# Moving the scaling and splitting of softplus results to a later place among the attention tiles

## The chip, the cores and the metric

The kernel runs on one core of a Trainium2 chip. The metric is the device time of one execution in microseconds (us). Engines are named as in the profile: PE (TensorE matmuls), PEld (TensorE weight loads), DVE (VectorE), ACT (ScalarE), POOL (GpSimd), SP (SyncE, which issues the DMAs). All of them run their own instructions in order and meet through semaphores.

## What is computed

Attention with a threshold, and behind it a feed-forward layer with softplus, all in float32 at the interface:

```
scores = scale * q @ k.T                      # 8 x 8 heads, 576 x 576, head size 64
thresh = max(scores, axis=-1) - tau
attn   = exp(where(scores >= thresh, scores, -1e9) - max)   # then divided by its row sum
x      = (attn @ v), heads side by side        # 4608 x 512
h = x @ w_in                                   # 4608 x 2048
g = max(h, 0) + log1p(exp(-abs(h)))            # softplus
out = g @ w_out                                # 4608 x 512
```

## The kernel before, in words

**Attention.** A unit is a pair of heads (32 units); a unit has 9 tiles of 128 query rows, so there are 288 tiles, counted here from 0 (tile 204 is the seventh of unit 22). A tile goes through: scores on PE (4 matmuls of 128x288 in float32, `scores`), the negated row maximum on DVE (`row_max`, tile `negm`), the exponentials on ACT with the threshold right behind them (`exps`, tiles `e_all` and `thr`), the mask on DVE (`mask`, written back to `e_all`, which also gives the row sums), and then the split of the weights into two float16 halves: the upper half on POOL (`weights_hi`) and the lower half on DVE (`weights_lo`), both in the tile that the profile calls `h`. These go through a DMA transpose (`weights_T`) and meet the values on PE (`values`, tile `pv`), whose result is copied by ACT and added by DVE into `xp`. There are two score banks (`SB = 2`): the scores of a tile can start only when the mask of the tile two before it has read its bank.

**Feed-forward.** The rows are taken in 10 chunks, eight of 512 rows and two of 256 (`chunks`; the last two form the tail, behind the attention). A chunk has 16 hidden blocks of 128 columns; `hidden` makes one by 12 matmuls from `xh`, `xl` and `w_i`. Two blocks at a time (a pair) go to `softplus` (line 737): ACT loads the softplus table, makes two softplus activations out of PSUM into `st`, and scales each in place by a power of two (`u.sg`). POOL then splits each `st` into `gh` and `gl` (`parts_of`, line 763, by `halves`, line 183): four POOL instructions a pair, called the parts here; the profile names their results `g`. `project` multiplies the parts by `w_o` into `o`, and DVE or ACT adds `o` into `acc`. A matmul chunk has 8 pairs; in the stretch where attention and feed-forward run together the first of a chunk's seven ordinary pairs stands alone, and the other six come in three twos, about 8.6 us apart within a two.

**The order.** Each tile writes its instructions by a string, `PAT = "RemhlTfpSxfvwp"`: row maximum (R, of the tile two ahead), exponentials (e, two ahead), mask (m, one ahead), upper half (h, one ahead), lower half (l, this tile), transposes (T), a share of the feed-forward matmuls (f), a point (p), scores (S, three ahead), extras of the unit (x: queries and keys of the next unit, values of the last), again f, v, w, and a second point (p). The first p is the middle of a tile. `defer(n, f)` puts a step at the n-th point from now; `now["p"]` counts points and is odd in a middle. From tile 36 on, ACT, DVE and POOL keep exactly the order in which the code writes their instructions (class `Queue`, whose calls are all recorded at line 160); PE and SP are ordered by the scheduler, by its own estimate of when an instruction can start.

A pair's `softplus` is written at the point after its last hidden matmul (`HD[0] = 1`), its scalings right with it, and its parts one point later (`HD[1] = 1`). While weights are still being prepared (`prep`), and for the last pair of a chunk (`u.n in waits`), the parts are put off further.

Of the kernel before, what the change touches and what calls it, by code (L numbers as in the profile page):

```python
# [54 lines left out]
HD = (1, 1)  # L55
# [11 lines left out]
def tile_kernel(ctx: ExitStack, tc: tile.TileContext, q, k, v, tau, w_in, w_out, out):  # L67
# [76 lines left out]
    now = {"p": 0, "tile": 0}  # L144
# [570 lines left out]
    def hidden(u, fc):  # L715

        g, f = divmod(fc, 4)
        need("i", g)
        h_scales(u, g)
        n = TC // u.T  # L720
        i = fc % n
        if i == 0:
            u.bank = ps_g.tile([P, TC], F32, tag="g", name=f"h_{u.n}_{fc}")
        bank = u.bank
        e = slice(f * P, (f + 1) * P)
        for cc in range(NCC):
            for m, (a, x) in enumerate(((0, u.h), (0, u.l), (1, u.h))):
                nc.tensor.matmul(bank[:, i * u.T:(i + 1) * u.T], wi[g, cc][:, a, e], x[cc], start=(cc == 0 and m == 0),  # L728
                                 stop=(cc == NCC - 1 and m == 2))
                if cc == NCC - 1 and m == 2 and i == n - 1:  # L730
                    u.full.append((fc + 1 - n, bank))
                    if len(u.full) == PAIR:
                        full, u.full = u.full, []
                        defer(HD[0], lambda: softplus(u, full))
                yield u.T / 512

    def softplus(u, full):


        ts, last_ = [], None  # L740
        with tc.high_priority(SPP):
            for fc, bank in reversed(full):
                t = fpool.tile([P, TC], F32, tag="st", bufs=NST, name=f"st_{u.n}_{fc}")
                i = act.activation(t, bank, AF.Softplus, scale=u.ch[:, fc // 4:fc // 4 + 1]).ins
                if last_ is not None:
                    tc.add_manual_dep(i, last_.name, mybir.DependencyInfo(
                        mybir.DependencyClass.NoSync, mybir.DependencyReason.DATA), reason="one table load")
                last_ = i
                ts.append((fc, t))
            for fc, t in reversed(ts):  # L750
                act.activation(t, t, AF.Copy, scale=u.sg[:, fc // 4:fc // 4 + 1])
        def parts():
            if u.n in waits:
                waits[u.n].append(parts)
                return
            for n, (fc, t) in enumerate(reversed(ts)):
                defer(n if prep else 0, lambda fc=fc, t=t: parts_of(u, fc, t))
        defer(HD[1], parts)

    waits = {}  # L760
    later_g = [0]

    def parts_of(u, fc, t):

        home, tags, bufs = (fpool, ("gh", "gl"), NG)
        if u.tail:
            spare = [("kT", "kT", 2), ("qT0", "qT1", 1), ("nat", "nat", 2), ("vt", "vt", 2)]
            i = later_g[0] % (NG + len(spare))
            later_g[0] += 1
            if i >= NG:  # L770
                *tags, bufs = spare[i - NG]
                home = apool
        gh, gl = [home.tile([P, TC], F16, tag=tags[i], bufs=bufs, name=f"g{i}_{u.n}_{fc}") for i in range(2)]
        halves(gh, gl, t)
        for i in range(TC // u.T):
            c = slice(i * u.T, (i + 1) * u.T)
            u.g[fc + i] = (gh[:, c], gl[:, c])
# [113 lines left out]
    def defer(n, f):  # L891
        if n == 0:
            f()
        else:
            later.append((now["p"] + n, f))
# [19 lines left out]
    for n, (main, b, from_) in enumerate(spans):  # L915
        u = Chunk()
# [16 lines left out]
    prep = []  # L933
    for kind, g in WL:
        for m in range(4):
            n = len(prep)
# [167 lines left out]
```

## Time and profile before

| what | value |
|---|---|
| median of 3 runs (lowest to highest) | 1295.86 us (1295.76 to 1297.07) |
| the profiled execution, its own time | 1297.34 us |
| its span from first to last instruction | 1295.6 us |
| busy: PE, DVE, ACT, POOL | 95%, 71%, 69%, 69% |
| mean granted TensorE clock | 0.996 |
| softplus pairs | 72 (144 activations) |

The span is 1.7 us shorter than the profiled execution's own time; the rest lies around the instructions. The median of the runs is 1.5 us below the profiled execution. In the rows of a timeline stand the start in us, the duration in us, the engine, line, operation, result and inputs, shapes and count, and in brackets the idle time before it with what ended it. In the rows of waits stand the waiting engine and tile, what it waited for, then us in total, times and the longest. In the tables of stretches stand the stretch, its length, and each engine's busy us.

### The profile page before, as it was taken

What the parts mean: (1) busy time and instruction counts of PE and PEld (TensorE: products, weight loads), DVE (VectorE), ACT (ScalarE), POOL (GpSimd) and SP (SyncE); (2) the same over time, 40 slices, a digit from 0 to 9 for tenths busy, and PEclk for the clock granted to TensorE, in tenths of its full rate; (3) what the DMA queues carried; (4) which work ended last, traced back from release to release, by engine and by line L of the source; (5) the groups of instructions that cost most, each with busy time, mean ns of one, the idle gap of its engine ahead of it and who ended that gap; (6) DMA issues with size and microseconds to landing.
All of it is one profiled execution on the core that took longest, in us unless ns stands there. A gap on an engine that the chain in (4) does not pass through costs nothing.

```text
span 1295.6 us, 21809 instructions
## 1 busy us (share of the span) xinstructions
PE 1230.8 (95%) x7173; PEld 745.1 (58%) x7173; DVE 925.7 (71%) x1735; ACT 900.2 (69%) x1723; POOL 893.1 (69%) x970
## 2 busy tenths in 40 slices
PE   5999988888999999999999999999999999999998
PEld 4655545455665565656565655666657755554455
DVE  5889878989777887878777977786677676640111
ACT  5877887877777777777777787768676767744321
POOL 2466788888876787778766886687667777564332
PEclk9999999999999999999999999999999999999999
DMA  4545357755876787768767776676557555420010
GB/s 130 160 143 148 111 129 169 177 116 125 185 144 146 137 178 154 154 139 175 145 146 145 165 153 147 144 149 155 130 122 165 124 123 108 100 65 17 1 41 17
DMA packets 368738, 167.92 MB, mean 130 GB/s; under 512 B 320208, under 2 KB 346224, under 8 KB 368624
## 3 DMA queue, kind: packets, MB, share of 16 engines
q1 hardware_dynamic: 368624, 166.52, 57.5%
q8 instruction: 57, 0.93, 0.3%
q14 instruction: 57, 0.47, 0.1%
HBM read 56.62 MB, written 10.63 MB: 52 GB/s over the span
## 4 chain that ended last, share of the span: by engine, by line
PE 35%; ACT 15%; POOL 10%; DVE 8%; issue 7%; DMA 5%; SPq 1%; POOLq 0%; DVEq 0%; ACTq 0%
PE o L792 14%; PE h L728 12%; PE s L493 5%; ACT st L160 5%; ACT L160 5%; POOL g L160 4%; PE pv L608 3%; DVE h L160 2%; ACT e_all L160 2%; POOL h L160 2%; DVE negm L160 2%; DVE e_all L160 2%; POOL xl L160 1%; DMA eT<-h 1%; DVE acc L160 1%
## 5 line engine op out<-in xcount | busy, mean ns | idle before, releaser
L792 PE MATMUL o<-w_o,g 128*128 128x512 f16 x1728 | 405.0, 380 | 2.1 <-DVE xp L160 1.2
L728 PE MATMUL h<-xh,w_i 128*128 128x512 f16 (+1 forms) x1280 | 361.3, 359 | 6.7 <-ACT sums_i L160 3.6
L160 POOL TENSOR_SCALAR h<-e_all 128x576 f16<-128x576 f32 x243 | 223.9, 924 | 112.3 <-DVE e_all L160 108.6
L160 ACT ACTIVATE e_all<-s,negm 128x576 f32<-128x576 f32 x288 | 213.6, 742 | 124.8 <-DVE negm L160 121.8
L160 DVE TENSOR_REDUCE negm<-s 128x1 f32<-128x576 f32 x288 | 215.2, 747 | 87.4 <-PE s L493 86.3
L160 DVE SCALAR_TENSOR_TENSOR e_all<-s,thr,e_all 128x576 f32<-128x576 f32 x288 | 232.8, 809 | 62.2 <-ACT thr L160 61.3
L728 PEld LDWEIGHTS <-w_i 128*128 128x128 f16 x1920 | 178.8, 98 | 170.2 <-issue 14.3
L792 PEld LDWEIGHTS <-g 128*128 128x128 f16 x1728 | 159.5, 98 | 174.1 <-issue 3.5
L160 DVE SCALAR_TENSOR_TENSOR h<-e_all,h 128x576 f16<-128x576 f32 x243 | 229.4, 944 | 26.5 <-POOL h L160 26.1
L728 PE MATMUL h<-xl,w_i 128*128 128x512 f16 (+1 forms) x640 | 230.3, 360 | 1.2 <-POOL xl L160 1.0
L160 POOL TENSOR_SCALAR g<-st 128x512 f16<-128x512 f32 x144 | 97.9, 680 | 165.8 <-ACT st L160 154.2
L160 POOL TENSOR_TENSOR g<-st,g 128x512 f16<-128x512 f32 x144 | 172.6, 1199 | 12.0
L493 PE MATMUL s<-kT,q 128*128 128x288 f32 x768 | 154.5, 329 | 16.5 <-DVE e_all L160 11.8
L160 DVE SCALAR_TENSOR_TENSOR acc<-o,c,acc 128x512 f32<-128x512 f32 x108 | 80.2, 742 | 124.6 <-PE o L792 124.2
L160 ACT ACT_TABLE_LOAD x119 | 152.7, 1283 | 2.1
L160 ACT ACTIVATE st<-h,c 128x512 f32<-128x512 f32 x144 | 91.1, 684 | 79.9 <-PE h L728 79.2
L493 PEld LDWEIGHTS s<-kT,q 128*128 128x128 f32 x768 | 116.4, 192 | 48.6 <-DVE e_all L160 31.5
L608 PE MATMUL pv<-eT,vt 128*128 128x288 f16 x972 | 139.9, 287 | 3.4 <-DVE xp L160 2.5
L493 PE MATMUL s<-kT,qT 128*128 128x288 f32 x512 | 106.8, 329 | 4.2 <-DVE e_all L160 3.8
L608 PEld LDWEIGHTS <-vt 128*128 128x128 f16 x972 | 88.7, 98 | 37.1 <-issue 5.0
L160 ACT COPY xp<-pv 64x288 f32<-64x288 f32 (+3 forms) x133 | 50.5, 383 | 78.8 <-PE pv L608 74.8
L160 ACT ACTIVATE st<-st,c 128x512 f32<-128x512 f32 x144 | 96.1, 714 | 2.3
(118 smaller groups left out, 1504.1 us busy)
## 6 DMA issues: line engine op xcount, KB each, us to landing
q<-q SPq DMA_DIRECT2D x62, 192.0 KB
kn<-in_k_dram SPq DMA_DIRECT2D x32, 256.0 KB
qn<-in_q_dram SPq DMA_DIRECT2D x32, 256.0 KB
vn<-in_v_dram SPq DMA_DIRECT2D x32, 256.0 KB
wc_i<-in_moe_w_in_dram SPq DMA_DIRECT2D x16, 512.0 KB
wc_o<-in_moe_w_out_dram SPq DMA_DIRECT2D x16, 512.0 KB
qT<-qT SPq DMA_DIRECT2D x62, 128.0 KB
out_dram<-acc SPq DMA_DIRECT2D x14, 512.0 KB
```

The costliest lines, as they stand in the source:

```text
L160: i = getattr(self.eng, name)(*args, **kwargs)
L493: nc.tensor.matmul(sp[:, hf, 0:HS], lhs, s.kT[j][:, hf * HS:(hf + 1) * HS], start=(m == 0), stop=(m == len(parts) - 1))
L608: nc.tensor.matmul(o[:, 0:HS], s.vt[:, a, :], s.eT[j][:, b, x0:x0 + HS], start=(n == 0), stop=(n == 2 * NC))
L728: nc.tensor.matmul(bank[:, i * u.T:(i + 1) * u.T], wi[g, cc][:, a, e], x[cc], start=(cc == 0 and m == 0), stop=(cc == NCC - 1 and m == 2))
L792: nc.tensor.matmul(o, u.g[fc][m // 2][:, sl], wo[fc][:, m % 2, :], start=(n == 0), stop=(n == 3 * QF - 1))
```

## The change

For a pair outside the tail, after the preparation of weights, and not among those that are put off, the scalings are no longer written with the softplus activations. They and the parts are both put at the next middle of a tile: one point on when the softplus was written at the end of a tile, two when it was written in a middle. A function `scaled` now holds the scalings.

```diff
                 last_ = i
                 ts.append((fc, t))
+
+        def scaled():
             for fc, t in reversed(ts):
                 act.activation(t, t, AF.Copy, scale=u.sg[:, fc // 4:fc // 4 + 1])
+
         def parts():
             if u.n in waits:
                 waits[u.n].append(parts)
                 return
             for n, (fc, t) in enumerate(reversed(ts)):
                 defer(n if prep else 0, lambda fc=fc, t=t: parts_of(u, fc, t))
-        defer(HD[1], parts)
+        if prep or u.tail or u.n in waits:
+            scaled()
+            defer(HD[1], parts)
+            return
+
+        n = 1 + now["p"] % 2
+        defer(n, scaled)
+        defer(n, parts)
```

In the built program 48 of the 72 pairs are moved. The instructions and their number are the same on ACT, POOL and DVE (table loads included); DVE's order does not change at all. Three places show the rest, all at one two of pairs in chunk 4: pair (6, 7), called A below, written around tile 203, and pair (8, 9), called B.

ACT at pair A, before. `st` are the softplus results, `c0` and `c2` their scales in and out, `e_all` the exponentials (of tiles 204 and 205 here), `xp`, `kT` and `q0` copies for PE:

```order
L160 ACTIVATE st_4_7_9451<-h_4_7_9397,c0_4_8570 128x512
L160 ACTIVATE st_4_6_9453<-h_4_6_9361,c0_4_8570 128x512
L160 ACTIVATE st_4_6_9453<-st_4_6_9453,c2_4_8572 128x512
L160 ACTIVATE st_4_7_9451<-st_4_7_9451,c2_4_8572 128x512
L160 COPY xp_21_9241<-pv_21_3_9461 64x288
L160 CAST kT_23_0_9426<-tr_23_0_2_9471 128x64
L160 ACTIVATE q0_97<-tr_23_0_2_9471,qscale_90 128x64 x2
L160 ACTIVATE q0_97<-tr_23_0_1_9474,qscale_90 128x512
L160 ACT_TABLE_LOAD
L160 ACTIVATE e_all_131<-s_0_132,negm_22_6_9502 128x576
L160 ACTIVATE thr_22_6_9503<-negm_22_6_9502,ntau_87 128x1
L160 ACTIVATE e_all_131<-s_1_133,negm_22_7_9538 128x576
```

The same place after:

```order
L160 ACTIVATE st_4_7_9451<-h_4_7_9397,c0_4_8570 128x512
L160 ACTIVATE st_4_6_9453<-h_4_6_9361,c0_4_8570 128x512
L160 COPY xp_21_9241<-pv_21_3_9459 64x288
L160 CAST kT_23_0_9426<-tr_23_0_2_9469 128x64
L160 ACTIVATE q0_97<-tr_23_0_2_9469,qscale_90 128x64 x2
L160 ACTIVATE q0_97<-tr_23_0_1_9472,qscale_90 128x512
L160 ACT_TABLE_LOAD
L160 ACTIVATE e_all_131<-s_0_132,negm_22_6_9492 128x576
L160 ACTIVATE thr_22_6_9493<-negm_22_6_9492,ntau_87 128x1
L160 ACTIVATE st_4_6_9453<-st_4_6_9453,c2_4_8572 128x512
L160 ACTIVATE st_4_7_9451<-st_4_7_9451,c2_4_8572 128x512
L160 ACTIVATE e_all_131<-s_1_133,negm_22_7_9538 128x576
```

The two scalings go behind the exponentials and the threshold of tile 204, and stay ahead of the exponentials of tile 205.

POOL from pair A to pair B, before. `h16` is the upper half of a tile's weights (tile 203 in the row behind A's parts, 204 in the next), `g0` and `g1` are the parts, `q2` the split queries of the next unit, and the `xp` row is `scale_x`, the multiplication by the row scales:

```order
L160 TENSOR_SCALAR h16_134<-e_all_131 128x576
L160 TENSOR_SCALAR g0_4_6_9487<-st_4_6_9453 128x512
L160 TENSOR_TENSOR g1_4_6_9488<-st_4_6_9453,g0_4_6_9487 128x512
L160 TENSOR_SCALAR g0_4_7_9491<-st_4_7_9451 128x512
L160 TENSOR_TENSOR g1_4_7_9492<-st_4_7_9451,g0_4_7_9491 128x512
L160 TENSOR_SCALAR h16_134<-e_all_131 128x576
L160 TENSOR_SCALAR q2_23_1_9525<-qn_23_9301 128x4x64
L160 TENSOR_TENSOR q2_23_1_9525<-qn_23_9301,q2_23_1_9525 128x4x64
L160 TENSOR_SCALAR h16_134<-e_all_131 128x576
L160 TENSOR_TENSOR xp_21_9241<-xp_21_9241,R_21_9400 128x576
L160 TENSOR_SCALAR g0_4_8_9576<-st_4_8_9556 128x512
```

The same stretch after:

```order
L160 TENSOR_SCALAR h16_134<-e_all_131 128x576 x2
L160 TENSOR_SCALAR g0_4_6_9510<-st_4_6_9453 128x512
L160 TENSOR_TENSOR g1_4_6_9511<-st_4_6_9453,g0_4_6_9510 128x512
L160 TENSOR_SCALAR g0_4_7_9514<-st_4_7_9451 128x512
L160 TENSOR_TENSOR g1_4_7_9515<-st_4_7_9451,g0_4_7_9514 128x512
L160 TENSOR_SCALAR q2_23_1_9525<-qn_23_9301 128x4x64
L160 TENSOR_TENSOR q2_23_1_9525<-qn_23_9301,q2_23_1_9525 128x4x64
L160 TENSOR_SCALAR h16_134<-e_all_131 128x576
L160 TENSOR_TENSOR xp_21_9241<-xp_21_9241,R_21_9400 128x576
L160 TENSOR_SCALAR h16_134<-e_all_131 128x576
L160 TENSOR_SCALAR g0_4_8_9593<-st_4_8_9556 128x512
```

The upper half of tile 203 passes A's parts and that of tile 205 passes B's. The upper half of tile 204 stays between the two pairs, behind A's parts and the two query splits, and ahead of the multiplication of `xp`.

PE at the scores of tile 208 (`s_0` from `q0`), before; `pv` are nine matmuls with the values of unit 22, of which the last two are shown:

```order
L608 LDWEIGHTS vt_22_9252
L608 MATMUL pv_22_0_9641<-eT_22_0_9356,vt_22_9252 128x288
L608 LDWEIGHTS vt_22_9252
L608 MATMUL pv_22_0_9641<-eT_22_0_9356,vt_22_9252 128x288
L792 LDWEIGHTS g1_4_6_9488
L792 MATMUL o_4_1_1_9614<-w_o1_2_2283,g1_4_6_9488 128x512
L493 MATMUL s_0_132<-kT_23_0_9426,q0_97 128x288 x4
L792 LDWEIGHTS g0_4_7_9491
```

After, where these scores stand ahead of all nine:

```order
L802 LDWEIGHTS g0_4_6_9510
L802 MATMUL o_4_1_1_9614<-w_o1_2_2283,g0_4_6_9510 128x512
L493 MATMUL s_0_132<-kT_23_0_9426,q0_97 128x288 x4
L608 LDWEIGHTS vt_22_9252
L608 MATMUL pv_22_0_9641<-eT_22_0_9356,vt_22_9252 128x288
L608 LDWEIGHTS vt_22_9252
L608 MATMUL pv_22_0_9641<-eT_22_0_9356,vt_22_9252 128x288
```

The scheduler puts the scores of tile 208 ahead of nine `pv` matmuls and one `o` matmul. It does the same at each such two of pairs in chunks 1 to 4, and in the second and third two of a chunk it also moves the scores of the next tile ahead by four `pv` matmuls. Elsewhere the scores move at a few places only, by at most as much.

## The prediction

> **What bounds the kernel now.** I began with the page, then read the table of stretches, the waits of one chunk, and last the timelines of the four engines at one two of softplus pairs.
>
> ```profile
> PE 1230.8 (95%) x7173; PEld 745.1 (58%) x7173; DVE 925.7 (71%) x1735; ACT 900.2 (69%) x1723; POOL 893.1 (69%) x970
> ```
>
> ```profile
> core 0: us, PE busy (x) PEld busy (x) DVE busy (x) ACT busy (x) POOL busy (x), PEclk, DMA share, GB/s
> 578.40:713.30 134.90, 132.37 (x778) 81.18 (x777) 108.54 (x203) 100.80 (x186) 102.81 (x113) 1.00 0.74 152
> 713.30:848.10 134.80, 132.26 (x778) 81.09 (x776) 108.45 (x203) 100.71 (x184) 102.70 (x112) 1.00 0.72 152
> ```
>
> PE is nearly full, and its order of work holds no slack: what a scores instruction waits, the whole kernel waits, since the feed-forward tail behind the attention is PE work too. A chunk of 36 tiles repeats within 0.1 us, so one place read closely stands for all of its kind. Four chunks (1 to 4, the 539 us before 848) run in this way. No other engine is full, but each works in order, so the waits say where they are late:
>
> ```profile
> POOL g L160 <- ACT st L160: 12.9, 8, 3.7
> DVE e_all L160 <- ACT thr L160: 8.7, 7, 1.9
> PEld s L493 <- DVE e_all L160: 5.5, 12, 1.0
> DVE h L160 <- POOL h L160: 3.4, 6, 1.2
> ```
>
> These are of the stretch 713.3 to 848.1. PE's scores wait for masks (5.5 us at the weight loads, which is a bound on what the change can win there), masks wait for exponentials that stand behind softplus on ACT, and POOL's parts wait for the scalings. The last row is small now; the forecast rests on its growing.
>
> **ACT: what the move gives.** At pair A of chunk 4 (softplus at 784.80):
>
> ```profile
> 784.80 1.26 ACT L160 ACTIVATE st<-h,c 128x512 f32<-128x512 f32 x2
> 786.10 1.33 ACT L160 ACTIVATE st<-st,c 128x512 f32<-128x512 f32 x2
> 787.46 0.39 ACT L160 COPY xp<-pv 64x288 f32<-64x288 f32 x1
> ...
> 790.40 0.74 ACT L160 ACTIVATE e_all<-s,negm 128x576 f32<-128x576 f32 x1
> ...
> 791.22 0.73 ACT L160 ACTIVATE e_all<-s,negm 128x576 f32<-128x576 f32 x1
> ...
> 797.86 0.74 ACT L160 ACTIVATE e_all<-s,negm 128x576 f32<-128x576 f32 x1
> ```
>
> The scalings hold ACT from 786.10 to 787.46, 1.36 us. Without them there, tile 204's exponentials start at 789.04; the scalings follow 0.82 later (791.22 - 790.40, exponentials and threshold), at 789.86; tile 205's exponentials start at 791.22 as before. So only tile 204 gains, and the first scaling comes 3.76 us later (789.86 - 786.10). At pair B tile 206 gains likewise: exponentials at about 796.6, threshold 0.9 later, at 797.5.
>
> **POOL: what the move costs.**
>
> ```profile
> 786.90 0.62 POOL L160 TENSOR_SCALAR g<-st 128x512 f16<-128x512 f32 x1 [3.67 <-ACT st L160]
> ...
> 790.56 0.67 POOL L160 TENSOR_SCALAR h<-e_all 128x576 f16<-128x576 f32 x1
> 791.19 0.40 POOL L160 TENSOR_SCALAR q<-qn 128x256 fp32r<-128x256 f32 x1
> ...
> 792.38 1.18 POOL L160 TENSOR_SCALAR h<-e_all 128x576 f16<-128x576 f32 x1
> 793.52 1.41 POOL L160 TENSOR_TENSOR xp<-xp,R 128x576 f32<-128x576 f32 x1
> ...
> 799.20 1.31 POOL L160 TENSOR_SCALAR h<-e_all 128x576 f16<-128x576 f32 x2
> 800.98 0.72 POOL L160 TENSOR_SCALAR vt<-vn 128x640 f16<-128x640 f32 x1 [0.47 <-ACT vn L160]
> ```
>
> The parts start 0.80 behind the first scaling (786.90 - 786.10), hence at 790.66, and their four instructions take 3.66 (790.56 - 786.90): until 794.3, or 794.9 if a lower half of 0.75 on DVE meets them. The upper half that passes them (tile 203) fits into the 3.67 us of idle time ahead of the parts and is free, and nothing on DVE waited for it. But the upper half of tile 204 stands behind the parts and the two query splits, which take 1.19 (792.38 - 791.19). It moves from 792.38 to about 796.1 and ends at 796.8 (0.67 for one alone).
>
> **DVE: where that lands.**
>
> ```profile
> 791.35 0.82 DVE L160 SCALAR_TENSOR_TENSOR e_all<-s,thr,e_all 128x576 f32<-128x576 f32 x1 [0.76 <-ACT thr L160]
> ...
> 793.73 0.81 DVE L160 SCALAR_TENSOR_TENSOR e_all<-s,thr,e_all 128x576 f32<-128x576 f32 x1
> ...
> 794.46 1.08 DVE L160 SCALAR_TENSOR_TENSOR h<-e_all,h 128x576 f16<-128x576 f32 x1
> ...
> 798.82 0.82 DVE L160 SCALAR_TENSOR_TENSOR e_all<-s,thr,e_all 128x576 f32<-128x576 f32 x1 [1.87 <-ACT thr L160]
> ...
> 802.36 0.80 DVE L160 SCALAR_TENSOR_TENSOR e_all<-s,thr,e_all 128x576 f32<-128x576 f32 x1
> ...
> 803.10 0.75 DVE L160 SCALAR_TENSOR_TENSOR h<-e_all,h 128x576 f16<-128x576 f32 x1
> ...
> 805.78 0.81 DVE L160 SCALAR_TENSOR_TENSOR e_all<-s,thr,e_all 128x576 f32<-128x576 f32 x1
> ```
>
> The masks are those of tiles 204, 205, 206, 207 and 208. Tile 204's comes up to 0.76 earlier. Behind 205's stands the lower half of 204 (794.46), and it needs the upper half that now ends at 796.8: DVE waits there for over 2 us, and behind it on DVE stand the row maximum of 207, the mask of 206 and all that follows. Its own length grows too, for POOL goes on to the `xp` multiplication at once. The same meeting is in the trace:
>
> ```profile
> 900.09 1.41 POOL L160 TENSOR_TENSOR xp<-xp,R 128x576 f32<-128x576 f32 x1
> ...
> 900.16 1.96 DVE L160 SCALAR_TENSOR_TENSOR h<-e_all,h 128x576 f16<-128x576 f32 x1 [1.03 <-POOL h L160]
> ```
>
> A lower half alone takes 0.75 (803.10); this one, started 0.07 behind the multiplication, took 1.96. So the lower half of 204 ends at 796.8 + 2.0 = 798.8; a row maximum takes 0.7, and the mask of 206 starts at 799.5, not earlier than its 798.82, although its threshold is ready at 797.5. SBUF — State Buffer of the Trainium skill, section Who interferes with whom, has a rule that speaks against this place: a VectorE instruction with two SBUF inputs and a GpSimd instruction that reads SBUF share a read port, and whichever comes first holds it for its whole length. The row of 1.96 agrees. If instead the lower half took 0.75 beside the multiplication, the mask of 206 would start at 798.3.
>
> **PE: the price.**
>
> ```profile
> 791.79 0.41 PE L433 MATMUL tr<-identr,k 128*128 128x128 f32 x1
> 792.23 0.78 PE L493 MATMUL s<-kT,qT 128*128 128x288 f32 x4
> 796.29 2.12 PE L792 MATMUL o<-w_o,g 128*128 128x512 f16 x9
> 798.25 1.27 PE L608 MATMUL pv<-eT,vt 128*128 128x288 f16 x9
> ...
> 799.70 0.79 PE L493 MATMUL s<-kT,q 128*128 128x288 f32 x4
> 803.23 0.79 PE L493 MATMUL s<-kT,q 128*128 128x288 f32 x4 [0.50 <-DVE e_all L160]
> 806.75 0.88 PE L493 MATMUL s<-kT,q 128*128 128x288 f32 x4
> ```
>
> Scores start 0.88 behind the start of the mask they wait for (799.70 - 798.82). What can be won: 0.3 at 792.23 (0.44 behind one transpose's start, where about 0.1 would do), and 0.6 at 803.23 (the idle 0.50 and the rest of the four matmuls' spacing), together 0.9. What it costs: tile 208's scores now stand ahead of the `pv` row, so PE reaches them at 798.25 less the 0.3 won, 797.95, and they can start at 799.5 + 0.88 = 800.4. PE waits 2.4 us. Less 0.9 that is 1.5. On DVE the delay is carried on: B's parts start behind the `xp` multiplication, the lower half and the upper half of 205, at about 799.5, and end near 803.8 (3.66, and 0.65 for a lower half between); the upper half of 206 ends at 804.4, its lower half meets POOL's value split (0.72) and ends at about 805.8 where 803.85 stood; the 1.93 us from there to the mask of 208 (805.78 - 803.85) remain, so that mask comes near 807.8, 2 us late. Its scores can start at 808.7; PE is there at 806.75 + 1.5 = 808.25, and waits 0.4 more. Price of a two: 1.9 us. For the first two of a chunk the same steps give 1.5, since its scores one tile on wait longest before (0.6) and are not moved.
>
> What I cost at nothing: the parts' readers on PE. A's last part ends at 794.9 and PE's first `o` that reads it stands in the row at 796.29, so 1.4 us cover it; beyond that each us of delay would be a us of PE. The SP queue, whose transposes and loads swap a few places, waits for halves that are later only by what is counted. Table loads stay as many.
>
> A pair alone (the first of a chunk) has its upper halves in front of its parts and no second pair behind it. There a wait goes:
>
> ```profile
> 750.90 1.26 PE L608 MATMUL pv<-eT,vt 128*128 128x288 f16 x9 [0.63 <-DVE xp L160]
> ```
>
> That `xp` addition stands behind a lower half which had waited for the upper half that now passes the parts; 0.6 us are won. From 848 to 1140 the tiles are longer, and PE waits little for masks:
>
> ```profile
> PEld s L493 <- DVE e_all L160: 2.4, 6, 0.9
> ```
>
> There a late upper half has cover. I take 0, from -2 (this row gone) to +4 (18 moved pairs, two tenths each), and also 0 for the one two of chunk 0, whose larger waits balance it.
>
> **The sum.** A chunk: 1.5 + 1.9 + 1.9 - 0.6 = 4.7 us; four chunks 18.8. On the profiled execution's 1297.34 us (span 1295.6) that is 1316.1 (span 1314.4); on the median of the runs, 1.5 lower, 1295.86 + 18.8 = 1314.7, which I give as 1314.5.
>
> **The rivals.** (1) The exponentials win. If the upper half of 204 is not what DVE waits for, every mask behind a pair is up to 1.36 earlier and PE loses its waits: 0.9 in each two, 0.6 at the lone pair, 3.3 a chunk, 13 us with four chunks, and up to 2 later: about 1282. For it speaks the 8.7 us that masks wait for thresholds; against it that POOL's order is fixed and the upper half stands behind 3.66 + 1.19 us of work that starts at 790.66. It decides at one point: an upper half of 204 that ends before 794.5. Chance 0.15. (2) The trade is even: the lower half is not held up by the multiplication (0.75 instead of 1.96), PE waits 1.2 instead of 2.4 at 208's scores and nothing at 210's. Then a two costs 1.2 - 0.9 = 0.3, a chunk 0.9 - 0.6, and the kernel stays within 2 us, about 1297. Against it stands the row at 900.16. Chance 0.15. (3) The parts come too late for `o`: if they slip by 2 us more than I count, PE loses some 0.6 at each of 28 pairs besides, about 17 us: 1331. Chance 0.05. That the build would not make the move is ruled out by its order.
>
> TensorE: Matmul & The Clock Gate, section Architectural detail, says that PE's queue pulls weight loads ahead of running matmuls, and names no matmul that passes a waiting one. The idle 0.50 at 803.23, with `pv` matmuls behind it, agrees. If matmuls did pass, the 2.4 us would be filled, and a two would cost nothing.
>
> **How the numbers follow.** The forecast has 0.65. Its own range comes from the bounds: a two between 1.0 and 2.6 (the mask of 206 half a us either way, with or without the 0.4 at 210), thus 12 x 1.0 - 2.4 - 2 = 8 to 12 x 2.6 - 2.4 + 4 = 33 us, mostly 8 to 28: 1304 to 1324. The range reaches to the even trade and leaves out rivals 1 and 3: 1293 to 1324. A measurement of this kernel can tell about 0.2%, 2.6 us, from no change. Faster by more: rival 1 and a little of rival 2, 0.17; within: most of rival 2, 0.13; slower: 0.70.
>
> **What would show it.** Right: in a chunk's stretch, DVE's lower halves waiting for POOL's upper halves for some 9 us instead of 3.4, among them waits of 2 us behind A's parts; the lower half there taking near 2 us; tile 208's scores idle for about 2 us; a chunk of 139 us instead of 134.8. The thresholds' wait should fall well under 8.7. Wrong: a chunk of 134.8 or less, or `o` matmuls that wait for POOL's parts, or growth that lies behind 848.

## The result, and the profile after

| | before | after |
|---|---|---|
| median of the runs (lowest to highest) | 1296.46 us (1295.76 to 1297.24) | 1318.16 us (1317.32 to 1318.98) |
| profiled execution: its own time, its span | 1297.34, 1295.6 us | 1317.88, 1316.1 us |
| softplus of pair A of chunk 4 | 784.80 | 800.97 |
| one matmul chunk (36 tiles) | 134.8 us | 139.0 us |

The changed kernel takes 1.0168 times as long (95% interval 1.0156 to 1.018): 21.7 us slower, against a forecast of 18.8. The two stretches below run from one chunk's last softplus to the next; the first numbers are the length and PE's busy time.

```profile
589.00:728.00 139.00, 132.82 (x779) 80.83 (x777) 112.82 (x203) 100.44 (x184) 105.80 (x113) 1.00 0.71 148
728.00:867.00 139.00, 132.84 (x779) 80.89 (x777) 112.79 (x203) 100.45 (x185) 105.80 (x113) 1.00 0.67 147
```

PE is busy nearly as long as before (132.84 against 132.26) in 4.2 us more: it waits. Of the 20.5 us that the span grew, chunks 1 to 4 hold 16.5, chunk 0 (its first softplus to its last) 3.4, the attention behind them, up to the third softplus of the last matmul chunk, 0.4, and the rest 1.3; the start is 1.1 us shorter. The waits of the second stretch, to be laid beside those of before (3.4, 5.5 and 1.6 us for the first three):

```profile
DVE h L160 <- POOL h L160: 12.0, 9, 2.5
PEld s L493 <- DVE e_all L160: 9.2, 13, 2.0
PE s L493 <- DVE e_all L160: 4.6, 3, 1.5
POOL g L160 <- ACT st L160: 12.1, 5, 3.5
```

The masks' wait for thresholds, 8.7 us before, is no longer in the list; the lower halves' wait for upper halves has grown from 3.4 to 12.0 us. At pair A one sees how. ACT first (start, duration, engine, operation): the scalings stand behind the exponentials of tile 204.

```profile
805.22 0.74 ACT L160 ACTIVATE e_all<-s,negm 128x576 f32<-128x576 f32 x1
...
806.04 1.32 ACT L160 ACTIVATE st<-st,c 128x512 f32<-128x512 f32 x2
807.27 0.72 ACT L160 ACTIVATE e_all<-s,negm 128x576 f32<-128x576 f32 x1
```

POOL, in the same kernel, stands idle 3.12 us for them (in brackets), and then runs without a gap to the upper half of 206 and beyond:

```profile
806.84 0.62 POOL L160 TENSOR_SCALAR g<-st 128x512 f16<-128x512 f32 x1 [3.12 <-ACT st L160]
...
812.14 0.67 POOL L160 TENSOR_SCALAR h<-e_all 128x576 f16<-128x576 f32 x1
812.78 1.41 POOL L160 TENSOR_TENSOR xp<-xp,R 128x576 f32<-128x576 f32 x1
814.15 1.18 POOL L160 TENSOR_SCALAR h<-e_all 128x576 f16<-128x576 f32 x1
815.30 0.61 POOL L160 TENSOR_SCALAR g<-st 128x512 f16<-128x512 f32 x1
...
819.45 0.67 POOL L160 TENSOR_SCALAR h<-e_all 128x576 f16<-128x576 f32 x1
```

DVE has made the mask of 205 (809.52), waits 2.51 us for the upper half of 204, and then has no gap either until it waits again, for the upper half of 206 (820.15). The four masks are those of 205, 206, 207 and 208:

```profile
809.52 0.81 DVE L160 SCALAR_TENSOR_TENSOR e_all<-s,thr,e_all 128x576 f32<-128x576 f32 x1
...
812.85 1.95 DVE L160 SCALAR_TENSOR_TENSOR h<-e_all,h 128x576 f16<-128x576 f32 x1 [2.51 <-POOL h L160]
...
815.39 0.80 DVE L160 SCALAR_TENSOR_TENSOR e_all<-s,thr,e_all 128x576 f32<-128x576 f32 x1
...
819.01 0.80 DVE L160 SCALAR_TENSOR_TENSOR e_all<-s,thr,e_all 128x576 f32<-128x576 f32 x1
...
820.15 1.26 DVE L160 SCALAR_TENSOR_TENSOR h<-e_all,h 128x576 f16<-128x576 f32 x1 [0.33 <-POOL h L160]
...
823.48 0.81 DVE L160 SCALAR_TENSOR_TENSOR e_all<-s,thr,e_all 128x576 f32<-128x576 f32 x1
```

And PE, which waits 0.22 us for POOL's late query splits and then stands idle 1.53 us ahead of the scores of 208:

```profile
812.23 0.54 PE L433 MATMUL tr<-identr,q 128*128 128x128 f32 x4 [0.22 <-POOL q L160]
...
816.25 0.80 PE L493 MATMUL s<-kT,q 128*128 128x288 f32 x4 [1.53 <-DVE e_all L160]
```

ACT, POOL and DVE went as forecast; PE waits less at the scores of 208 than the 2.4 us of the forecast. In chunks 1 to 4 together the idle time of PE's matmuls grew from 10.3 to 25.5 us: scores that wait for masks from 6.2 to 18.3 us (1.5 at each of 12 twos), transposes that wait for query splits from 0 to 5.6, while 2.5 us at `pv` are gone. One measure serves below: how far the mask of 208 lies behind A's softplus. It was 20.98 us before (805.78 - 784.80) and is 22.51 now (823.48 - 800.97), 1.5 us late.

### The profile page after: what moved, and what is told of

Same layout as the page of the kernel before. It is cut to its first block, busy times and chain, and to the rows that moved or that the text cites. A ratio compares the mean times of both kernels' runs of the same rounds, so it can differ in the third digit from the quotient of the medians.

```text
span 1316.1 us, 21811 instructions
## 1 busy us (share of the span) xinstructions
PE 1233.4 (94%) x7173; PEld 744.9 (57%) x7173; DVE 949.2 (72%) x1735; ACT 896.2 (68%) x1723; POOL 905.1 (69%) x970
## 4 chain that ended last, share of the span: by engine, by line
PE 51%; POOL 12%; issue 6%; ACT 5%; DVE 5%; DMA 1%; POOLq 0%; SPq 0%; ACTq 0%; DVEq 0%
PE h L728 19%; PE o L802 16%; PE s L493 7%; POOL g L160 6%; PE pv L608 6%; POOL h L160 2%; ACT L160 2%; PE tr L433 1%; ACT st L160 1%; POOL xl L160 1%; POOL q L160 1%; DVE negm L160 1%; DVE h L160 1%; DVE e_all L160 1%; ACT e_all L160 1%
## 5 line engine op out<-in xcount | busy, mean ns | idle before, releaser
L160 DVE SCALAR_TENSOR_TENSOR h<-e_all,h 128x576 f16<-128x576 f32 x243 | 253.7, 1044 | 64.2 <-POOL h L160 63.7
L728 PEld LDWEIGHTS <-w_i 128*128 128x128 f16 x1920 | 179.7, 98 | 170.0 <-issue 14.7
L160 POOL TENSOR_SCALAR g<-st 128x512 f16<-128x512 f32 x144 | 103.1, 716 | 163.3 <-ACT st L160 159.8
L160 POOL TENSOR_TENSOR g<-st,g 128x512 f16<-128x512 f32 x144 | 181.3, 1259 | 12.0
L608 PE MATMUL pv<-eT,vt 128*128 128x288 f16 x972 | 138.4, 287 | 4.0 <-ACT qT L160 2.4
```

The lines of the kernel that those rows point to most:

```text
L160: i = getattr(self.eng, name)(*args, **kwargs)
L608: nc.tensor.matmul(o[:, 0:HS], s.vt[:, a, :], s.eT[j][:, b, x0:x0 + HS], start=(n == 0), stop=(n == 2 * NC))
```

## The experiments

The theory: the late scalings stop POOL, which keeps its order; the upper half of 204 stands behind A's parts, the lower half of 204 waits for it and is held by the multiplication, and PE, given the scores of 208 too early, pays. Rivals: POOL's new order is the loss by itself; PE's new order is; the scalings behind the exponentials make ACT late. Ratios are to the kernel before; the chunk is chunk 4, the second stretch above (134.8 before).

| run | median, us | ratio (95%) | a chunk, us |
|---|---|---|---|
| only the parts moved | 1290.86 | 0.9963 (0.995 to 0.9975) | 133.5 |
| only A moved | 1345.15 | 1.0384 (1.037 to 1.0399) | 146.8 |
| only B and the lone pair moved | 1303.25 | 1.0064 (1.0051 to 1.0078) | 135.0 |
| after, `pv` ahead of the scores of 208 | 1318.02 | 1.0172 (1.0158 to 1.0186) | 139.0 |
| after, multiplication one point later | 1318.65 | 1.0173 (1.0152 to 1.0194) | 138.9 |
| before, multiplication one point later | 1313.51 | 1.0135 (1.0116 to 1.0153) | 138.3 |
| after, parts one more tile later | 1302.27 | 1.0046 (1.0028 to 1.0064) | 135.1 |
| scalings in place, parts as late | 1319.90 | 1.0182 (1.0163 to 1.0201) | 138.4 |
| scalings half way | 1280.60 | 0.9884 (0.9867 to 0.9902) | 131.6 |
| mixed | 1295.21 | 0.9995 (0.9985 to 1.0004) | 134.5 |
| after, multiplication on DVE | 1314.05 | 1.0137 (1.0115 to 1.0159) | 137.2 |
| before, multiplication on DVE | 1306.42 | 1.008 (1.0057 to 1.0103) | 136.4 |

**Only the parts moved.**

```diff
-        defer(n, scaled)
+        scaled()
         defer(n, parts)
```

> The scalings stay with the softplus activations; only the parts go to the next middle. POOL's order is then that of the changed kernel instruction by instruction (the upper half of 204 behind A's parts), and PE's order is that of the kernel before. Theory (the loss is the upper half of 204 coming late because A's parts wait for late scalings, met by scores that PE has been given too early): the scalings are done at once, so A's parts start right behind the upper half of 203, at most 0.7 us later than before, and the upper half of 204 is late by at most that; within 3 us of the kernel before, 1293 to 1298. Rival, POOL's order alone is the loss: near the changed kernel, 1310 to 1318.

Measured 1290.86 us. POOL's order is that of the changed kernel, and the loss is gone; it is even a gain of 0.4%. POOL, then DVE, at the same two:

```profile
779.29 1.12 POOL L160 TENSOR_SCALAR h<-e_all 128x576 f16<-128x576 f32 x1 [3.22 <-DVE e_all L160]
780.37 0.61 POOL L160 TENSOR_SCALAR g<-st 128x512 f16<-128x512 f32 x1
...
785.20 1.18 POOL L160 TENSOR_SCALAR h<-e_all 128x576 f16<-128x576 f32 x1
```

```profile
787.32 1.05 DVE L160 SCALAR_TENSOR_TENSOR h<-e_all,h 128x576 f16<-128x576 f32 x1
```

The parts follow the upper half of 203 without a wait, and the lower half of 204 (787.32) waits for nothing. Most of the gain lies behind B: the upper half of 205 now passes B's parts, and the lower half of 205 has neither the 0.26 us wait nor the length of 1.21 that it had before. (Some 0.4 us a chunk come from the lone pair, where `pv` waits 0.21 us instead of 0.63.) That POOL's order is the loss is ruled out; what is left between this kernel and the changed one is the place of the scalings, and PE's order, which the scheduler makes from it; together they are 27 us.

**Only A moved, and only B and the lone pair moved.** `full[0][0] % 4` is 0 for B and the lone pair and 2 for A; the second run has the condition without `== 0`.

```diff
-        if prep or u.tail or u.n in waits:
+        if prep or u.tail or u.n in waits or full[0][0] % 4 == 0:
             scaled()
```

> Only the first pair of each two (A) is moved; the second and the lone pair stay as before. POOL then holds the upper half of 204 behind late parts as in the changed kernel, but PE's scores of 208 stay behind the nine pv matmuls. Theory: DVE's lower half of 204 waits as long as in the changed kernel (2.5 us, and near 2 us of its own), the mask of 206 comes about 0.4 us later than before, and PE has pv matmuls to do in the meantime: +0.1 to +0.5 us a two, 1296 to 1302. Rival, the late upper half alone costs the whole price whatever PE's order: 1308 to 1318.

> Only the second pair of each two (B) and the lone pair are moved; A stays as before. PE's order is then that of the changed kernel (scores of 208 ahead of nine pv matmuls), while the upper half of 204 is not behind late parts. Theory: the mask of 206 follows its earlier threshold, the scores of 208 wait 0.3 us or less, and some 0.6 us a two are won: 1286 to 1297. Rival, the early scores are the loss by themselves (whatever comes before them, PE reaches them 1.1 us too soon): +1 us a two, 1305 to 1312. Second rival, the scalings behind the exponentials make ACT late: slower than before by more than 3 us, with growing waits of ACT or of masks for thresholds.

Both expectations failed. Moving A alone costs 49.5 us (1345.15 - 1295.68), more than twice the whole change. The wait for the upper half of 204 is the same 2.51 us, but here B's parts still stand ahead of the upper half of 205, so a second one follows (DVE), and PE meets it at a `pv` whose bank waits for DVE's addition of `o` into `acc`, queued behind:

```profile
838.33 1.94 DVE L160 SCALAR_TENSOR_TENSOR h<-e_all,h 128x576 f16<-128x576 f32 x1 [2.51 <-POOL h L160]
...
844.48 1.21 DVE L160 SCALAR_TENSOR_TENSOR h<-e_all,h 128x576 f16<-128x576 f32 x1 [2.81 <-POOL h L160]
```

```profile
846.40 0.99 PE L608 MATMUL pv<-eT,vt 128*128 128x288 f16 x4 [2.13 <-DVE acc L160]
```

The theory had counted the first wait and forgotten that the same lateness meets the next upper half. PE's scores were not moved in this kernel, and it lost most. With B alone moved, PE's scores stand as early as in the changed kernel and a chunk takes 135.0, as before: early scores are no loss by themselves. By its number the run falls to the second rival (slower by more than 3 us), but not by that rival's sign: the masks' waits for thresholds shrank, from 8.7 to 2.9 us in chunk 4. There is no gain in the chunks either, since B's late scalings stop POOL too, with the upper half of 206 behind. The three rows are of POOL, DVE and PE:

```profile
799.60 0.62 POOL L160 TENSOR_SCALAR g<-st 128x512 f16<-128x512 f32 x1 [2.05 <-ACT st L160]
```

```profile
804.34 1.26 DVE L160 SCALAR_TENSOR_TENSOR h<-e_all,h 128x576 f16<-128x576 f32 x1 [1.46 <-POOL h L160]
```

```profile
806.01 0.28 PE L426 MATMUL tr<-identr,k 128*128 128x128 f32 x1 [0.69 <-DVE xp L160]
```

Chunks 1 to 4 are even here, and most of the 7.6 us lies elsewhere: 4.1 in chunk 0 and 2.4 in the attention behind the chunks.

**PE's order.** At the eighth tile of a unit the extras go ahead of the scores, so that nine `pv` matmuls stand ahead of the scores of 208 again.

```diff
-        for step in PAT:
+        for step in PAT if t != 7 else PAT.replace("Sx", "xS"):
```

> The changed kernel, with the scores of a tile written behind the values of the unit at the eighth tile of a unit, so that nine pv matmuls (about 1.1 us) stand ahead of the scores of 208 again. Theory: DVE and POOL wait as in the changed kernel, but 1.1 of the 1.8 us that PE waits there are filled: 12 twos by about 1.1 are 13 us less, 1303 to 1308. Rival, PE's order is beside the point because the mask of 206 sets the pace of every later step: within 3 us of the changed kernel, 1315 to 1321.

Measured 1318.02: nothing won. My theory fell here. PE's wait moves one tile on, from 1.53 us at 208 to 0.43 there and 0.87 at 209:

```profile
815.90 0.80 PE L493 MATMUL s<-kT,q 128*128 128x288 f32 x4 [0.43 <-DVE e_all L160]
...
819.53 0.79 PE L493 MATMUL s<-kT,q 128*128 128x288 f32 x4 [0.87 <-DVE e_all L160]
```

The mask of 208 stands at 823.12, 22.5 us behind A's softplus (800.6), as in the changed kernel. What PE does in between makes no difference here; the masks set the pace.

**The held lower half.** `XD` 9 instead of 8 puts the multiplication behind the upper half of 205; the control does the same to the kernel before.

```diff
-XD = 8
+XD = 9
```

> The changed kernel, with the multiplication of xp by the row scales put one point later, so that on POOL the upper half of 205 stands between the upper half of 204 and the multiplication. The upper half of 204 is as late as before (DVE waits 2.5 us for it). Theory with the port (the lower half of 204 is held by whatever POOL runs at its start): it meets an upper half of 0.67 instead of a multiplication of 1.41, takes 1.3 instead of 1.95, and the lower half of 205 is not held either: 0.6 to 1.5 us a two, 1300 to 1311. Rival, the 2.5 us of waiting alone make the price and the length of the lower half does not count: 1315 to 1321.

> Control: the kernel before, with the multiplication one point later. It stands there ahead of the upper half of 205 as well or behind it, and behind B's parts; no lower half waits long there. Every theory: within 4 us of the kernel before, 1292 to 1300.

The first falls into its rival's range, and the control missed. In the changed kernel the lower half of 204 is held less, as expected, and the mask of 206 is 0.7 us nearer to A's softplus (814.69 - 801.0 = 13.7 instead of 14.4). But nothing is won, for DVE then waits longer for the upper half of 206, and the mask of 208 is 22.4 us behind A's softplus:

```profile
812.89 1.21 DVE L160 SCALAR_TENSOR_TENSOR h<-e_all,h 128x576 f16<-128x576 f32 x1 [2.52 <-POOL h L160]
...
820.08 1.26 DVE L160 SCALAR_TENSOR_TENSOR h<-e_all,h 128x576 f16<-128x576 f32 x1 [1.46 <-POOL h L160]
```

PE's wait only moves: 0.78 us at the scores of 208, and 0.70 at a transpose behind the late lower half of 206. The control was no control: the multiplication now falls on the lower half of 205, which takes 1.96 instead of 1.21 there (and that of 207 takes 1.33 instead of 0.75), and a chunk takes 3.5 us more.

```profile
812.28 1.42 POOL L160 TENSOR_TENSOR xp<-xp,R 128x576 f32<-128x576 f32 x1
```

```profile
812.35 1.96 DVE L160 SCALAR_TENSOR_TENSOR h<-e_all,h 128x576 f16<-128x576 f32 x1 [0.27 <-POOL h L160]
```

So a held lower half can cost PE on its own, where DVE alone is late; in the changed kernel POOL is as late as DVE, and freeing one leaves the other.

**Later parts.** A's parts then stand behind the upper half of 204; POOL does not stop for scalings. The second run has ACT's order of the kernel before with the same POOL order.

```diff
-        defer(n, parts)
+        defer(n + 2, parts)
```

```diff
-        defer(n, scaled)
-        defer(n, parts)
+        scaled()
+        defer(n + 2, parts)
```

> The changed kernel, with the parts one more tile later than the scalings: POOL never waits for a late scaling with an upper half behind it, since A's parts come behind the upper half of 204 and the query splits. ACT's order is that of the changed kernel. Theory (what costs is POOL standing idle for late scalings with the upper half of 204 behind it): DVE's wait of 2.5 us and its held lower half go, and with them the whole loss: 1284 to 1296. Rival, ACT: the scalings behind the exponentials are the loss by themselves: 1308 to 1320. Second rival, the third of the prediction: the parts come too late for the o matmuls, which then wait for POOL: 1298 to 1330, with idle time of o released by g.

> Scalings with the softplus activations as in the kernel before, parts one more tile later than in the changed kernel. Against the kernel with only the parts moved (1290.9) this shows what late parts cost by themselves: Theory: their readers have 5 us and more of slack, so 1287 to 1295. Rival, late parts hold up o: 1298 and more, with idle time of o released by g.

With late scalings and later parts 16 us of the loss go (1302.27), though not all: it lies outside the theory's range and inside the second rival's. ACT's order is that of the changed kernel, so the scalings behind the exponentials are not the loss. What remains is mostly the prediction's third rival, first of POOL, then of PE:

```profile
792.80 0.61 POOL L160 TENSOR_SCALAR g<-st 128x512 f16<-128x512 f32 x1
```

```profile
795.81 0.61 PE L802 MATMUL o<-w_o,g 128*128 128x512 f16 x2 [0.58 <-POOL g L160]
```

The parts of A come 0.6 us too late for `o`. In the whole run `o` waits 25 times for POOL's parts, 13.2 us together, where it never waits in the kernel before; gains at other places hide a part of that (a chunk takes 135.1 us, where it took 134.8). The other run missed, on the rival's side: 1319.90, with `o` waiting twice (0.28 and 0.70 us) at each A, because the upper half of 204, ahead of these parts, comes with the later exponentials. The two have one POOL order and differ in the scalings' place (and, by the scheduler, in the place of a few scores, which the run on PE's order showed to be worth nothing in the changed kernel), and there late scalings win 17.6 us. The gain on ACT that the change was after is real; it is spent on POOL.

**Scalings half way.** The scalings are written directly ahead of the next tile's exponentials, behind the copies that ACT makes for PE; the parts as in the changed kernel.

```diff
         def parts():
+            while pend:
+                pend.pop(0)()
...
-        n = 1 + now["p"] % 2
-        defer(n, scaled)
-        defer(n, parts)
+        pend.append(scaled)
+        defer(1 + now["p"] % 2, parts)
...
+    pend = []
...
             elif step == "e" and ahead:
+                while pend:
+                    pend.pop(0)()
```

> POOL's order is that of the changed kernel; the scalings are written directly ahead of the next tile's exponentials, behind the copies that ACT makes in between (1.7 us at A). Against the kernel with only the parts moved, the first scaling of A is about 1.75 us later instead of 3.8, and POOL waits for it about 1.1 us instead of 3.1. Theory (POOL runs without a gap from the late parts on, and only what its wait exceeds its slack of some 1.3 us costs): little or nothing, 1288 to 1295. Rival, every us of a later scaling costs alike: 1.1/3.1 of the 27 us between the kernel with only the parts moved and the changed kernel, 1299 to 1303.

Measured 1280.60, 1.2% under the kernel before and below both expected ranges: the best of all. POOL waits for A's scaling, but not long enough to cost anything, and PE is busy 131.29 of 131.60 us:

```profile
775.06 0.62 POOL L160 TENSOR_SCALAR g<-st 128x512 f16<-128x512 f32 x1 [0.88 <-ACT st L160]
```

```profile
781.11 1.95 DVE L160 SCALAR_TENSOR_TENSOR h<-e_all,h 128x576 f16<-128x576 f32 x1
```

```profile
701.30:832.90 131.60, 131.29 (x779) 80.64 (x778) 110.43 (x203) 100.02 (x186) 106.43 (x113) 1.00 0.74 155
```

The lower half of 204 is held for the same 1.95 us, and it is hidden: DVE has no wait in front of it and a wait for a threshold (1.46 us) behind it. The gain over the kernel with only the parts moved, 1.9 us a chunk, fits the copies, which now pass the scalings: the addition into `xp` had waited 0.84 us for ACT's copy there and no longer does. The expectation had left that out, and no run tries it by itself. Loss is therefore not in proportion to lateness: 0.88 us of waiting costs nothing, 3.12 us cost 5.5 us a chunk (139.0 against 133.5).

**Mixed.** B and the lone pair in chunks 0 to 4 with late scalings and later parts, all others as with only the parts moved.

```diff
-        defer(n, scaled)
+        if u.n < 5 and full[0][0] % 4 == 0:
+            defer(n, scaled)
+            defer(n + 2, parts)
+            return
+        scaled()
         defer(n, parts)
```

> In chunks 0 to 4 the lone pair and B have their scalings at the next middle and their parts one more tile later, so that POOL never waits for these scalings; A and all later pairs have scalings in place and parts at the next middle. Theory: the exponentials behind B's softplus come 1.36 us earlier and POOL is not stopped for it, and B's parts have the slack for it: 1281 to 1289. Rival, the parts of B come too late for o, or the upper half of 206 is late again: 1293 to 1305, with idle time of o released by g, or lower halves that wait over 1 us.

The theory failed: 1295.21, no change from before and within the rival's range. `o` has no wait for B's parts, but they and the value splits now stand ahead of the upper half of 207, for which DVE waits:

```profile
803.32 1.21 DVE L160 SCALAR_TENSOR_TENSOR h<-e_all,h 128x576 f16<-128x576 f32 x1 [1.22 <-POOL h L160]
```

The slack of the parts' readers was not the bound on B's parts; the next upper halves were.

**The multiplication on DVE.**

```diff
-        pool.tensor_tensor(out=s.xp, in0=s.xp, in1=s.R, op=ALU.mult)
+        vec.tensor_tensor(out=s.xp, in0=s.xp, in1=s.R, op=ALU.mult)
```

> The changed kernel with the multiplication of xp by the row scales made by DVE, 1.41 us of POOL's work behind the upper half of 204 taken away and about 0.75 given to DVE ahead of the next row maximum. DVE's wait of 2.5 us for the upper half of 204 stays. Theory (POOL's gapless run from the late parts to the upper half of 206 sets the pace): about 1 to 1.4 us a two, 1301 to 1308. Rival, DVE's wait for the upper half of 204 sets the pace: 1314 to 1325.

> Control: the kernel before, with the multiplication made by DVE. POOL stands idle there ahead of A's parts in any case. Every theory: within 5 us of the kernel before, 1291 to 1301.

The changed kernel wins 4 us by it (1314.05), which is the near edge of the rival's range; the control loses 10 us, more than expected: the multiplication, 1.2 us long, now stands in DVE's queue. With the multiplication on DVE the change costs 7.6 us instead of 22. That speaks for POOL's work behind the late parts as part of the price, but two engines' loads change at once, and I do not count it as shown.

## Why the prediction was right, point by point

**ACT.** Right. Tile 204's exponentials come 4.25 us behind the start of A's softplus (805.22 - 800.97), where 4.24 was forecast, and the first scaling 5.07 behind it, where 5.06 was. Thresholds are no longer waited for.

**POOL.** Right: parts 5.87 us behind A's softplus (forecast 5.86), the upper half of 204 done at 11.84 (forecast 12.0).

**DVE.** Right: a wait of 2.51 (over 2), a lower half of 1.95 (1.96 by the quoted meeting), the mask of 206 at 14.42 (forecast 14.7). The rule of the shared read port from SBUF — State Buffer of the Trainium skill, section Who interferes with whom, agrees at this place again: 1.95 beside a multiplication, 1.21 beside an upper half of 0.67, and 0.75 alone.

**PE.** The price came out near, 4.2 us a chunk against 4.7, but the step behind it was wrong in its reason. The prediction let the scores of 208 wait 2.4 us because they stand ahead of nine `pv` matmuls; the rows show 1.53 idle, and with the `pv` matmuls put back ahead of them nothing is won. The difference of 0.9 has two parts: the mask of 206 comes 0.3 sooner than forecast, and PE arrives 0.6 later, above all because its transposes wait for the query splits behind the late parts, a reader that the prediction did not list. The 0.4 us at 210 did not come. The step to replace it: DVE and POOL run almost without a gap behind the late upper half of 204 (DVE stops once more, for 0.33 us), the mask of 208 comes 1.5 us later for it, and PE pays that once, wherever it meets the late masks. By that step the forecast would have been 3 x 1.5 a chunk, and the 0.9 a two counted as won would have been left out.

**The even trade** (the lower half not held) and the exponentials' win did not happen, and the runs show why: the lower half is held, but even where it is held less the chunk stays at 138.9; the gain on ACT exists (17.6 us between the two runs with later parts), but only where POOL waits little or not at all for the scaling.

**The lone pair.** Wrong by its size. The 0.6 us at `pv` are won, and the query splits behind the late parts take them back: PE's transposes of the queries wait (0.77).

```profile
767.23 0.28 PE L428 MATMUL tr<-identr,q 128*128 128x128 f32 x1 [0.77 <-POOL q L160]
```

**Chunk 0.** Wrong: forecast 0, measured 3.4. POOL splits prepared weights (`w_o`) there, behind the late parts; ACT, in order, waits for that, with the copies for PE behind it (ACT, then PE):

```profile
292.52 0.72 ACT L160 ACTIVATE w_o<-wa_o,wscale_o 128x512 f16<-128x512 f32 x1 [4.81 <-POOL w_o L160]
```

```profile
294.62 1.26 PE L608 MATMUL pv<-eT,vt 128*128 128x288 f16 x9 [2.37 <-ACT qT L160]
```

It is the same fault as at A, with another passenger: the prediction listed what POOL has behind the parts at one two and took the others to be alike.

**Behind the chunks.** Forecast 0 (-2 to +4), measured 1.7 from the last softplus of chunk 4 to the end.

**The total.** That it came within 3 us of the forecast is in part luck: where the forecast put its 18.8 us the runs show 16.5, the waits there are other ones than it added up, and chunk 0 makes up the rest. (Chunks 1 to 4 take 540 us in the kernel before, not 539.)

What stays open is how the 1.5 us of a two divide between POOL's chain and DVE's: where DVE's lower half was held less, POOL's chain stayed, and the run that took the multiplication from POOL loaded DVE.

## What to carry to other kernels

When a step is moved behind other work on one engine, look at its reader first: on an engine that keeps its order, a reader that has to wait stops everything queued behind it, and that, not the reader, is the price. The best place was neither end but the one where the reader had just come free: behind the copies that PE waits for and ahead of the exponentials. A stall that two in-order engines shared was not had back here by holding one of them less (1318.65 us) or by giving PE other work meanwhile (1318.02); taking work off the other won 4 of 22 us.

## What the runs showed of the hardware that was not expected

**The granted clock after a short stop.** In chunk 0 of the changed kernel PE stood idle for 2.37 us, and the clock that it was granted (third number from the end) then fell to half, for some 6 us by the shares below:

```profile
294.50:298.50 4.00, 3.04 (x15) 2.15 (x15) 2.74 (x6) 3.92 (x8) 3.03 (x3) 0.70 0.38 88
298.50:302.20 3.70, 3.70 (x10) 1.39 (x9) 3.48 (x7) 1.74 (x4) 3.38 (x4) 0.50 0.71 168
```

The hidden matmuls started 0.43 us apart there (298.80 to 299.23) instead of 0.22. The 1.53 us stops at each two left the clock at 1.00, while the kernel with only A moved, with one stop of 2.9 and two of 2.1 us in a chunk, ran its chunks at 0.97. There such a stop is paid for twice: chunks 1 to 4 take 47.7 us more than before, but PE's idle time in them grew by only 30.6 us, and about 3% of their 588 us, lost to the clock, are 17.6 us more.

Yet the length of a stop does not settle it. With the scalings in place and the parts as late, PE stood idle for 2.93 us in chunk 0, and the clock stayed at 1.00, with the next hidden matmul 0.22 us behind the first:

```profile
296.71 0.38 PE L728 MATMUL h<-xh,w_i 128*128 128x512 f16 x1 [2.93 <-DVE xp L160]
296.93 0.38 PE L728 MATMUL h<-xl,w_i 128*128 128x512 f16 x1
```

Other stops in chunk 0 of 2.22 us (later parts) and 2.70 us (changed kernel, multiplication one point later) left it at 1.00 too, while one of 2.04 us (mixed) halved it; of two stops of 1.93 us near the end of the attention, one halved it (changed kernel, multiplication on DVE) and one did not (`pv` ahead of the scores). So between 1.9 and 2.9 us it went either way, and what decides is not shown. TensorE: Matmul & The Clock Gate of the Trainium skill, section Part 1: The HAM clock gate, tells of such halving after an idle window of about 3.4 us; here shorter stops were at times enough.

**Who is held.** The holding works both ways: with the multiplication started behind a waiting lower half, it is the multiplication that lasts 1.91 us instead of 1.41 (POOL, in the changed kernel with the multiplication one point later).

```profile
813.46 1.91 POOL L160 TENSOR_TENSOR xp<-xp,R 128x576 f32<-128x576 f32 x1
```
